# Performer attention and an MLP-mixer on one core: VectorE's maxima, reciprocals and head scalings as jobs of their own, some of the scalings on other engines, and a new order

## The chip, the core and the metric

The kernel runs on one core of a Trainium2 chip. The core has a matrix engine (TensorE, "PE", with its weight loads as "PEld"), three engines for elementwise work (VectorE "DVE", ScalarE "ACT", GpSimd "POOL") and a queue engine (SyncE "SP") that issues transfers. Every engine takes its instructions in the order in which the program holds them. TensorE writes its products into eight banks of PSUM, from which DVE and ACT read them.

The metric is device time of one execution in microseconds (us), the median of the runs. Before the change it is 279.47 us over three runs (279.39 to 279.99).

## The reference

Attention with random features comes first, for 8 batches of 8 heads with 576 rows of 64 numbers. Its result, 512 numbers for each row, goes through a mixer: a two-layer network over the rows and then one over the 512 channels, each with what went in added to what comes out.

```python
def phi(x):                                  # x: q or k, times 64 ** -0.25
    h = x @ omega.T - (x * x).sum(-1, keepdims=True) / 2
    return np.exp(h - h.max(-1, keepdims=True)) / np.sqrt(128)
q_p, k_p = phi(q_s), phi(k_s)
kv = np.einsum('bhsm,bhsd->bhmd', k_p, v)
num = np.einsum('bhsm,bhmd->bhsd', q_p, kv)
den = np.einsum('bhsm,bhm->bhs', q_p, k_p.sum(2))[..., None] + 1e-06
x = (num / den)                              # heads side by side: [8, 576, 512]
h = np.maximum(x.transpose(0, 2, 1) @ w_tok1, 0) @ w_tok2
u = x + h.transpose(0, 2, 1)
out = u + np.maximum(u @ w_ch1, 0) @ w_ch2
```

## The kernel before

**Tiling.** Of each batch's 576 rows, 512 lie as four blocks of 128 on the partitions; the last 64 (the tail) are handled with those of another head or batch. Products run in fp16 with fp32 sums.

**Attention** (`attention`, from L564) goes by pairs of heads. PE projects k (L699) and q (L711, tail rows L661 and L594), ACT takes the exponentials (L557). For k the row's maximum is divided out after the exponential: DVE takes the maximum over 128 features (L723, `km`), its reciprocal (L725) goes into a 65th column of `vs`, and POOL multiplies v by that column (L731, shown at the helper's L306). PE multiplies (L744, tail rows L751 or L753), a copy brings the product to SBUF (`kvsb`), and PE forms numerator and denominator of one head in one bank (L777, tail L779). The head scaling follows: DVE takes the reciprocal of the denominators, five numbers in each partition (L786), and multiplies five blocks of 64 by them (L787) into `x`. In batch 0 alone, two heads are multiplied by ACT (L799), which takes five instructions, one for each block.

**Mixer.** `token_mix` multiplies `x` by the first weights (L813, L820), a relu goes to `r`, the second product (L833) is added to `x` by DVE (L836), and a transfer on SP turns the result around (L841). Batch 0 has its own form in smaller pieces (L859 on). The tails of two batches go together (L887, DVE's sum L893). In `channel_mix` the first layer is L1120 (four matmuls and a relu for each of 12 blocks) and the second L965, for batch 0 L1155. The second layer uses a scheme with seven instead of eight products for batches 1 on, whose weight sums (`T`, L490) and operand sums (`S`, `r` at L306) DVE makes; from batch 6 on the first layer does too (L1053).

**Order.** Every piece of work is a job: `add(engine, cost, key, fn, deps, take, give)`. Nothing is scheduled when the program is built. `ORDER` is a list of job numbers, and the program is written out in exactly that order; a negative number is one 512-column matmul on zeros, which keeps PE's clock up (L1193). `SLOT` says which buffer of its ring a job takes. `MOVED` gives the engine for a job by its number, where it isn't the usual one (`engine`, L174). Relus and copies have ACT or DVE as their choice, the scaling of v POOL or DVE. Costs and keys play no part any more.

Of the kernel before, what the change touches and what calls it, by code (L numbers as in the profile page):

```python
# [9 lines left out]
FP32 = mybir.dt.float32  # L10
# [57 lines left out]
]  # L68
SLOT = (
# [110 lines left out]
def kernel(  # L180
# [12 lines left out]
    nc = tc.nc  # L193
# [28 lines left out]
    def ring(n, shape, dt, name):  # L222
        return [sb(shape, dt, f"{name}{i}") for i in range(n)]

    COUNT = {"qT": 3, "kT": 3, "v": 3, "vt": 2, "qp": 4, "kp": 4, "vs": 4, "qpt": 2, "kpt": 2, "vbd": 2,
             "kvsb": 3, "ktt": 2, "x": 3, "r1": 3, "u": 3, "uT": 3, "r3": 2, "S": 1, "V": 1, "s": 3, "o": 2, "bank": 8}
    plan = Planner(COUNT)
    place = plan.place
    engine = plan.engine
# [996 lines left out]
```

## Time and profile before

| what | us |
|---|---|
| median of three runs | 279.47 (279.39 to 279.99) |
| the profiled execution | 279.72 |
| its span, from the first instruction to the last | 277.9 |
| PE busy | 265.6 |
| DVE busy | 233.7 |
| ACT busy | 154.5 |
| POOL busy | 91.6 |
| mean granted clock of TensorE | 0.974 of full speed |

Busy time is the time in which at least one instruction of that engine ran. Matmuls overlap one another, so PE's share says that it had work and not that it ran at its peak. A wait is counted where an engine stood idle for more than 0.15 us, and is put down to the engine whose result came last.

### The profile page before, as it was taken

Reading aid. Unit: us, or ns where it says so; the run is one execution under the profiler, and the core shown is the slowest. Engines: PE = TensorE matmul, PEld = TensorE weight load, DVE = VectorE, ACT = ScalarE, POOL = GpSimd, SP = SyncE. Lnnn points to the kernel's source line nnn. Section 1 sums busy time; section 2 is a strip of 40 time slices with the busy share of each in tenths; the row PEclk is TensorE's granted clock in tenths of the full one; section 3 lists DMA queues with packets and bytes.
Section 4 is the critical chain, followed back from the end, with each engine's and each line's share of the span. In section 5 each row is a group of like instructions: output and inputs, shape, how many; then the busy total and the mean of one; then the engine's idle time right before and its main releaser. Section 6 shows DMA issues by size and latency. Waiting matters only on the chain.

```text
span 277.9 us, 6547 instructions
## 1 busy us (share of the span) xinstructions
PE 265.6 (96%) x2624; PEld 179.5 (65%) x2624; DVE 233.7 (84%) x487; ACT 154.5 (56%) x318; POOL 91.6 (33%) x115
## 2 busy tenths in 40 slices
PE   5789999999999999999999999999999999999993
PEld 2657546443657755665677646764597688888882
DVE  1698828499999889996998799999997999889992
ACT  2797994049667427644567544878835425153410
POOL 8597794007510773048006910333400000000000
PEclk9559999999999999999999999999999999999999
DMA  7999999999997999995989993970060062030125
GB/s 160 200 205 169 182 185 204 164 151 211 182 226 164 164 211 162 170 196 89 189 181 211 203 195 85 167 179 4 18 174 0 2 150 97 0 153 0 65 105 136
DMA packets 80622, 39.69 MB, mean 143 GB/s; under 512 B 63984, under 2 KB 76144, under 8 KB 80400
## 3 DMA queue, kind: packets, MB, share of 16 engines
q0 software_dynamic: 31696, 17.61, 44.0%
q1 hardware_dynamic: 47696, 18.52, 30.5%
q10 hardware_dynamic: 1200, 3.15, 3.2%
q8 instruction: 20, 0.33, 0.5%
q14 instruction: 10, 0.08, 0.1%
HBM read 35.95 MB, written 16.52 MB: 189 GB/s over the span
## 4 chain that ended last, share of the span: by engine, by line
PE 88%; DVE 4%; DMA 3%; ACT 2%; issue 1%; ACTq 0%; DVEq 0%
PE bank L965 25%; PE bank L1120 22%; PE bank L1053 9%; PE bank L833 5%; PE bank L820 5%; PE bank L1155 4%; PE bank L711 3%; PE bank L699 3%; DMA wc<-in_k_dram 3%; PE bank L777 3%; PE bank L744 2%; DVE o L954 1%; PE bank L887 1%; DVE x L787 1%; PE bank L859 1%; ACT qp L557 1%
## 5 line engine op out<-in xcount | busy, mean ns | idle before, releaser
L301 ACT ACTIVATE r<-bank 128x512 f16<-128x512 f32 (+1 forms) x82 | 46.3, 604 | 43.5 <-PE bank L1120 25.6
L1120 PE MATMUL bank<-uT,wc 128*128 128x512 f16 x280 | 67.9, 379 | 0.0
L306 POOL TENSOR_TENSOR vs<-v,vs 128x512 f16<-128x512 f16 x32 | 34.3, 1072 | 79.5 <-DVE vs L725 49.8
L1120 PEld LDWEIGHTS <-wc 128*128 128x128 f16 x280 | 24.8, 98 | 25.7 <-issue 2.6
L965 PEld LDWEIGHTS <-r 128*128 128x128 f16 x384 | 36.7, 98 | 6.9 <-issue 1.3
L557 ACT ACTIVATE qp<-bank 128x512 f16<-128x512 f32 x64 | 36.6, 624 | 8.0 <-PE bank L711 5.2
L557 ACT ACTIVATE kp<-bank 128x512 f16<-128x512 f32 x64 | 36.5, 617 | 7.2 <-PE bank L699 7.0
L723 DVE TENSOR_REDUCE km<-kp 128x8 f16<-128x1024 f16 x32 | 38.5, 1205 | 0.6 <-ACT kp L557 0.4
L787 DVE TENSOR_TENSOR x<-bank,rc 128x320 f16<-128x320 f32 x62 | 30.5, 492 | 2.1
L965 PEld LDWEIGHTS <-S 128*128 128x128 f16 x288 | 28.2, 98 | 5.3 <-issue 0.6
L999 POOL DMA_DIRECT2D out_dram<-o x1 | 0.7, 665 | 73.4 <-issue 73.4
L965 PE MATMUL bank<-T,r 128*128 128x256 f16 x192 | 23.8, 273 | 0.0
L965 PE MATMUL bank<-wc,r 128*128 128x256 f16 x192 | 23.6, 273 | 0.0
L965 PE MATMUL bank<-T,S 128*128 128x256 f16 x192 | 23.6, 273 | 0.0
L303 DVE TENSOR_SCALAR r<-bank 128x512 f16<-128x512 f32 (+1 forms) x26 | 17.1, 663 | 7.5 <-PE bank L820 4.9
L954 DVE TENSOR_TENSOR o<-u,bank 128x512 f32<-128x512 f16 x28 | 19.0, 679 | 2.8 <-PE bank L965 2.6
L836 DVE TENSOR_TENSOR u<-x,bank 128x512 f16<-128x512 f16 x28 | 17.6, 680 | 0.5 <-ACT r L297 0.5
L777 PEld LDWEIGHTS <-qp 128*128 128x128 f16 x256 | 13.7, 100 | 6.2 <-issue 0.2
L954 DVE TENSOR_TENSOR o<-o,bank 128x512 f32<-128x512 f32 (+1 forms) x25 | 15.1, 612 | 2.7 <-PE bank L965 2.5
L1053 PEld LDWEIGHTS <-wc 128*128 128x128 f16 x144 | 13.8, 98 | 2.6 <-issue 0.6
L777 PE MATMUL bank<-kvsb,qp 128*128 128x65 f16 x256 | 15.0, 196 | 0.0
L711 PE MATMUL bank<-qT,omT 64*128 64x512 f16 x64 | 12.5, 410 | 1.7 <-ACT qT L297 1.7
(151 smaller groups left out, 470.5 us busy)
## 6 DMA issues: line engine op xcount, KB each, us to landing
out_dram<-o SPq DMA_DIRECT2D x10, 512.0 KB, 2.9
q<-in_q_dram POOLq DMA_DIRECT2D x6, 576.0 KB, 9.6
wc<-in_moe_w_ch_dram POOLq DMA_DIRECT2D x4, 768.0 KB, 10.8
k<-in_k_dram POOLq DMA_DIRECT2D x6, 512.0 KB, 7.8
v<-in_v_dram POOLq DMA_DIRECT2D x6, 512.0 KB, 10.0
out_dram<-o ACTq DMA_DIRECT2D x4, 512.0 KB, 2.7
r<-in_q_dram POOLq DMA_DIRECT2D x4, 288.0 KB, 7.1
v<-in_v_dram POOLq DMA_DIRECT2D x4, 256.0 KB, 9.5
```

The source lines that it names most:

```text
L301: nc.scalar.activation(out=out, in_=in_, func=AF.Relu)
L306: (nc.gpsimd if eng == "POOL" else nc.vector).tensor_tensor(**kw)
L557: nc.scalar.activation(out=out, in_=in_, func=AF.Exp, bias=0.0, scale=1.0)
L711: nc.tensor.matmul(ps[e], omT[half[e]], t[half[e], 2 * hp : 2 * hp + 2, 0:R], start=True, stop=True)
L723: nc.vector.reduce_max(out=mx, in_=kpv, axis=AX.X)
L777: nc.tensor.matmul(ps[:, k, j * 65 : (j + 1) * 65], st, s[:, i, 0 : D + 1], start=True, stop=True)
L787: nc.vector.tensor_tensor(out=t_x[place("x", b)][:, :, (2 * hp + hs[0]) * D : (2 * hp + hs[0] + n) * D].rearrange("p j (i d) -> p i j d", ...
L836: nc.vector.tensor_tensor(out=t_u[place("u", b)][:, j, :], in0=t_x[place("x", b)][:, j, :], in1=bank(n), op=ALU.add)
L954: nc.vector.tensor_tensor(out=o, in0=a, in1=ps, op=ALU.add)
L965: nc.tensor.matmul(ps[:, j * DH : (j + 1) * DH], a[:, cb, j * P : (j + 1) * P], w[:, cb, :], start=(bank_of(b, j0) not in held and j == j0 ...
L1053: nc.tensor.matmul(ps[:, 2 * P * t : 2 * P * t + 2 * P], a_[:, k, cb * P : (cb + 1) * P], m[:, :, k, :], start=(begin and t == 0 and k == ...
L1120: nc.tensor.matmul(ps, wc1[:, db, cb * P : (cb + 1) * P], moving(db), start=(db == 0), stop=(db == ND - 1))
```

## The change

Five things are altered in the code.

1. DVE's two or three instructions for one thing, which stood together in one job, become jobs of their own: the maximum of k and its reciprocal, the maximum, reciprocal and mask product of the tail rows, the reciprocal of a head's denominators and the head scaling, and the two halves of the sum for two batches' tails. Others can now stand between them.
2. Each head scaling can go to DVE or ACT. In batch 0 the same two heads have ACT as their usual engine; with `MOVED`, 24 of the 64 heads are ACT's (2 before) and 40 DVE's.
3. Seven of 32 scalings of v are DVE's; all were POOL's.
4. There are four buffers for the maxima (`km`) instead of two, and six for a head's reciprocals (`rc`) instead of four of twice the size.
5. `ORDER`, `SLOT` and `MOVED` are new throughout. Ten warming matmuls are left of 13. Ten more relus from PSUM are DVE's, and ACT has six more in SBUF.

```diff
-             "kvsb": 3, ... "o": 2, "bank": 8}
+             "kvsb": 3, ... "o": 2, "km": 4, "rc": 6, "bank": 8}
...
             def km(hp=hp):
                 kpv = t_kp[place("kp", (b, hp))].rearrange("p c e m -> p (c e) m")
-                mx, vs = t_km[hp % 2], t_vs[place("vs", (b, hp))]
-                nc.vector.reduce_max(out=mx, in_=kpv, axis=AX.X)
+                nc.vector.reduce_max(out=t_km[place("km", (b, hp))], in_=kpv, axis=AX.X)
+            j_m = add("DVE", 1.2, at_["km"], km, deps=je, take=[("km", (b, hp))])
+            def km_rec(hp=hp):
                 with nc.allow_low_precision(reason="fp16 operand of the matmul"):
-                    nc.vector.reciprocal(out=vs[:, :, D], in_=mx)
-            j_m = add("DVE", 1.4, at_["km"], km, deps=je, take=[("vs", (b, hp))])
+                    nc.vector.reciprocal(out=t_vs[place("vs", (b, hp))][:, :, D], in_=t_km[place("km", (b, hp))])
+            j_m = add("DVE", 0.2, at_["km"], km_rec, deps=[j_m], take=[("vs", (b, hp))], give=[("km", (b, hp))])
...
-                    nc.vector.reciprocal(out=rc, in_=ps[:, :, :, D])
-                    nc.vector.tensor_tensor(
...
+                def rec(where=where, rc_of=rc_of):
+                    nc.vector.reciprocal(out=rc_of(), in_=where()[:, 0, 0 : 5 * 65].rearrange("p (j d) -> p j d", d=65)[:, :, D])
...
+                j_r = add("DVE", 0.22, kno - 0.3, rec, deps=[j_n], take=[n_rc])
+                e_no = engine(*("ACT", "DVE") if b == 0 and BY["no"][2 * hp + hs[0]] == "A" else ("DVE", "ACT"))
+                def num_out(hp=hp, i=hs[0], where=where, rc_of=rc_of, e_no=e_no):
+                    to = t_x[place("x", b)][:, :, (2 * hp + i) * D : (2 * hp + i + 1) * D]
+                    ps = where()[:, 0, 0 : 5 * 65].rearrange("p (j d) -> p j d", d=65)[:, :, 0:D]
+                    if e_no == "DVE":
+                        nc.vector.tensor_tensor(out=to, in0=ps, in1=rc_of().unsqueeze(2).broadcast_to((P, NJ + 1, D)), op=ALU.mult)
+                        return
+                    for j in range(NJ + 1):
+                        nc.scalar.activation(out=to[:, j], in_=ps[:, j], func=AF.Copy, scale=rc_of()[:, j : j + 1])
+                last_x.append(add(e_no, 0.62, kno, num_out, deps=[j_r], take=[("x", b)], give=[at, n_rc]))
```

What moves is seen only in the engines' own order. In the rows below a line number, the operation, what it writes and reads (with the buffer's number) and the shape follow one another. Line numbers of the changed kernel are nine to some 25 higher: its L801 is L786 or L796 here, its L809 L787, its L812 L799, its L736 and L740 the maximum L723 and its reciprocal L725, its L499 L490, its L306, L312 and L315 the helpers' L297, L303 and L306.

The first place is DVE where batch 0's first heads are scaled (`x_118`), some 19 us into the span. Before:

```order
L297 CAST kvsb_116<-bank_66 128x2x65
L297 COPY kT_88<-bank_68 128x576
L297 COPY kT_88<-bank_70 128x576
L796 RECIPROCAL rc_141<-bank_66 128x5
L786 RECIPROCAL rc_143<-bank_69 128x5
L787 TENSOR_TENSOR x_118<-bank_69,rc_143 128x5x64
L786 RECIPROCAL rc_143<-bank_64 128x5
L787 TENSOR_TENSOR x_118<-bank_64,rc_143 128x5x64
```

After:

```order
L315 TENSOR_TENSOR vs_105<-v_90,vs_105 128x8x64
L801 RECIPROCAL rc_143<-bank_63 128x5
L801 RECIPROCAL rc_144<-bank_70 128x5
L740 RECIPROCAL vs_106<-km_137 128x8
L306 COPY kT_88<-bank_68 128x576
L809 TENSOR_TENSOR x_118<-bank_63,rc_143 128x5x64
L801 RECIPROCAL rc_145<-bank_64 128x5
L809 TENSOR_TENSOR x_118<-bank_64,rc_145 128x5x64
```

A copy of `kvsb` and one of `kT` have left DVE, a scaling of v has come, and the reciprocal of a maximum and a copy now stand between a head's reciprocal and its scaling.

The second place is DVE where batch 2's attention begins, some 64 us into the span, with the weight sums `T` (L490). Before:

```order
L723 TENSOR_REDUCE km_135<-kp_99 128x8
L725 RECIPROCAL vs_103<-km_135 128x8
L490 TENSOR_TENSOR T<-wc_81,T 128x1536
L490 TENSOR_TENSOR T<-wc_81 128x1536
L303 TENSOR_SCALAR r_131<-bank_63 128x512
L723 TENSOR_REDUCE km_135<-kp_101 128x8
L725 RECIPROCAL vs_106<-km_135 128x8
L723 TENSOR_REDUCE km_134<-kp_102 128x8
L725 RECIPROCAL vs_104<-km_134 128x8
L303 TENSOR_SCALAR r_131<-bank_64 128x512
L490 TENSOR_TENSOR T<-wc_81,T 128x1536
```

After:

```order
L740 RECIPROCAL vs_104<-km_134 128x8
L740 RECIPROCAL vs_106<-km_135 128x8
L902 TENSOR_TENSOR ut<-x_118,bank_67 64x512
L736 TENSOR_REDUCE km_136<-kp_102 128x8
L312 TENSOR_SCALAR r_131<-bank_70 128x512
L499 TENSOR_TENSOR T<-wc_81,T 128x1536
L306 CAST kvsb_115<-bank_68 128x2x65
L740 RECIPROCAL vs_105<-km_136 128x8
L736 TENSOR_REDUCE km_137<-kp_101 128x8
L312 TENSOR_SCALAR r_131<-bank_69 128x512
```

One weight sum is left here, behind the first relu `r_131`, with a copy of `kvsb` right behind it; two have moved up, into batch 1's token mix.

The third place is ACT where batch 2's heads (`x_120`) are scaled among the relus `r_131` of batch 1's channel mix. Before:

```order
L301 ACTIVATE r_131<-bank_68 128x512
L301 ACTIVATE r_131<-bank_66 128x512
L297 CAST kvsb_117<-bank_63 128x2x65
L297 CAST kvsb_116<-bank_64 128x2x65
L301 ACTIVATE r_131<-bank_70 128x512
L301 ACTIVATE r_131<-bank_67 128x512
L297 CAST kvsb_115<-bank_65 128x2x65
```

After:

```order
L310 ACTIVATE r_131<-bank_70 128x512
L812 ACTIVATE x_120<-bank_65,rc_146 128x64 x5
L812 ACTIVATE x_120<-bank_67,rc_148 128x64 x5
L306 CAST kvsb_115<-bank_65 128x2x65
L310 ACTIVATE r_131<-bank_68 128x512
L310 ACTIVATE r_131<-bank_70 128x512
L812 ACTIVATE x_120<-bank_67,rc_143 128x64 x5
L310 ACTIVATE r_131<-bank_66 128x512
```

Three heads of batch 2, five instructions each, now stand between these relus.

More of the change, by code (lines that the diff above doesn't have):

```diff
@@ L76 @@
 )
 MOVED = {
-43: "ACT", 51: "ACT", 54: "ACT", 60: "ACT", 63: "ACT", 65: "ACT", 75: "DVE", 85: "ACT", 129: "ACT", 139: "DVE", 141: "DVE", 145: "ACT", 147: "DVE",
-163: "ACT", 169: "DVE", 171: "ACT", 175: "DVE", 179: "ACT", 190: "ACT", 194: "ACT", 228: "ACT", 242: "DVE", 256: "DVE", 265: "DVE", 278: "DVE", 280:
-"DVE", 286: "DVE", 300: "DVE", 324: "ACT", 399: "DVE", 426: "DVE", 428: "DVE", 432: "DVE", 434: "DVE", 484: "DVE", 498: "DVE", 552: "DVE", 556: "DVE",
-562: "DVE", 593: "ACT", 594: "ACT", 634: "DVE", 662: "DVE", 690: "DVE", 692: "DVE", 700: "DVE", 702: "DVE", 768: "DVE", 796: "DVE", 864: "ACT", 972:
@@ L82 @@
-"DVE", 988: "DVE", 1003: "ACT", 1105: "DVE", 1125: "DVE", 1127: "DVE", 1134: "DVE", 1157: "DVE", 1165: "ACT", 1203: "DVE", 1233: "DVE", 1242: "ACT",
-1244: "ACT", 1282: "SP", 1283: "SP", 1285: "ACT", 1286: "SP", 1287: "ACT", 1288: "SP", 1289: "ACT", 1290: "SP", 1291: "ACT", 1292: "SP",
+43: "ACT", 51: "ACT", 54: "ACT", 56: "ACT", 59: "ACT", 62: "ACT", 65: "ACT", 66: "ACT", 75: "DVE", 86: "ACT", 106: "DVE", 120: "ACT", 135: "DVE", 137:
+"ACT", 149: "DVE", 159: "ACT", 165: "DVE", 167: "DVE", 173: "ACT", 189: "ACT", 194: "ACT", 206: "DVE", 225: "DVE", 230: "ACT", 242: "DVE", 244: "ACT",
@@ new lines @@
+247: "ACT", 261: "DVE", 264: "ACT", 267: "ACT", 278: "DVE", 289: "DVE", 305: "DVE", 313: "DVE", 319: "DVE", 323: "DVE", 349: "ACT", 381: "ACT", 395:
+"DVE", 418: "ACT", 432: "ACT", 459: "DVE", 461: "DVE", 463: "DVE", 467: "DVE", 473: "DVE", 532: "ACT", 558: "DVE", 560: "DVE", 563: "ACT", 575: "DVE",
+580: "ACT", 583: "ACT", 586: "DVE", 604: "DVE", 610: "DVE", 620: "DVE", 647: "ACT", 675: "DVE", 714: "ACT", 717: "ACT", 726: "DVE", 728: "DVE", 731:
+"ACT", 737: "DVE", 752: "DVE", 758: "DVE", 762: "DVE", 768: "DVE", 862: "ACT", 865: "ACT", 876: "DVE", 879: "ACT", 901: "DVE", 909: "DVE", 911: "DVE",
@@ new lines @@
+915: "DVE", 979: "ACT", 1013: "ACT", 1027: "DVE", 1057: "DVE", 1069: "DVE", 1078: "DVE", 1088: "DVE", 1090: "DVE", 1098: "ACT", 1099: "ACT", 1100:
+"ACT", 1101: "ACT", 1111: "DVE", 1154: "DVE", 1160: "ACT", 1174: "ACT", 1191: "ACT", 1205: "DVE", 1211: "ACT", 1216: "DVE", 1237: "DVE", 1246: "DVE",
+1251: "DVE", 1265: "DVE", 1276: "ACT", 1278: "ACT", 1315: "DVE", 1331: "DVE", 1345: "DVE", 1353: "ACT", 1354: "ACT", 1355: "ACT", 1356: "ACT", 1393:
+"ACT", 1394: "SP", 1395: "SP", 1397: "ACT", 1398: "SP", 1399: "ACT", 1400: "SP",
@@ L225 @@
     COUNT = {"qT": 3, "kT": 3, "v": 3, "vt": 2, "qp": 4, "kp": 4, "vs": 4, "qpt": 2, "kpt": 2, "vbd": 2,
-             "kvsb": 3, "ktt": 2, "x": 3, "r1": 3, "u": 3, "uT": 3, "r3": 2, "S": 1, "V": 1, "s": 3, "o": 2, "bank": 8}
+             "kvsb": 3, "ktt": 2, "x": 3, "r1": 3, "u": 3, "uT": 3, "r3": 2, "S": 1, "V": 1, "s": 3, "o": 2, "km": 4, "rc": 6, "bank": 8}
     plan = Planner(COUNT)
@@ L271 @@
     t_o = ring(COUNT["o"], [P, 2, DM], FP32, "o")
-    t_km = ring(2, [P, 8], FP16, "km")
+    t_km = ring(COUNT["km"], [P, 8], FP16, "km")
     t_kmt = ring(2, [P, 4], FP16, "kmt")
@@ L275 @@
     t_rct = ring(2, [P, 4], FP16, "rct")
-    t_rc = ring(4, [P, 2, NJ + 1], FP32, "rc")
+    t_rc = ring(COUNT["rc"], [P, NJ + 1], FP32, "rc")
     nat = {}
@@ L562, in vbd_of @@
         return first_vbd[:, b] if b < NPE else t_vbd[place("vbd", b)]
+    kt_parts = {}
     def attention(b, key, step):
@@ L629, in attention, with kt_red, kt_rec, kt_vb @@
                 j_kte.append(add("ACT", 0.3, kkt, kt_exp, deps=[j_kt], take=[("kpt", b)], give=[("bank", (n_kt, e))]))
-            def kt_max():
-                kp = t_kpt[place("kpt", b)].rearrange("p g e m -> p (g e) m")
-                mx, rc, vb = t_kmt[b % 2], t_rct[b % 2], vbd_of(b)
-                nc.vector.reduce_max(out=mx, in_=kp, axis=AX.X)
+            def kt_red():
+                nc.vector.reduce_max(out=t_kmt[b % 2], in_=t_kpt[place("kpt", b)].rearrange("p g e m -> p (g e) m"), axis=AX.X)
+            j_ktm = add("DVE", 0.7, kkt + 0.01, kt_red, deps=[*j_kte, *kt_parts.get(b - 2, [])])
+            def kt_rec():
                 with nc.allow_low_precision(reason="fp16 operand of the matmul"):
-                    nc.vector.reciprocal(out=rc, in_=mx)
+                    nc.vector.reciprocal(out=t_rct[b % 2], in_=t_kmt[b % 2])
+            j_ktr = add("DVE", 0.2, kkt + 0.01, kt_rec, deps=[j_ktm])
+            def kt_vb():
                 nc.vector.tensor_tensor(
-                    out=vb[:, :, 0:nh, D],
-                    in0=rc.unsqueeze(2).broadcast_to((P, 4, nh)),
+                    out=vbd_of(b)[:, :, 0:nh, D],
+                    in0=t_rct[b % 2].unsqueeze(2).broadcast_to((P, 4, nh)),
                     in1=msk.unsqueeze(1).broadcast_to((P, 4, nh)),
@@ L641, in kt_max @@
                 )
-            j_ktm = add("DVE", 1.2, kkt + 0.01, kt_max, deps=[*j_kte, j_msk], take=[("vbd", b)] if dma_in else [])
+            j_ktm = add("DVE", 0.2, kkt + 0.01, kt_vb, deps=[j_ktr, j_msk], take=[("vbd", b)] if dma_in else [])
+            kt_parts[b] = [j_ktr, j_ktm]
             def vbd():
@@ L781, in attention @@
                           give=[("qp", (b, hp)), ("kvsb", (b, hp)), ("qpt", b)])
-                def num_out(hp=hp, hs=hs, where=where):
-                    n = len(hs)
-                    ps = where()[:, :, 0 : 5 * 65].rearrange("p i (j d) -> p i j d", d=65)
-                    rc = t_rc[2 + hp % 2][:, hs[0] : hs[0] + n]
-                    nc.vector.reciprocal(out=rc, in_=ps[:, :, :, D])
-                    nc.vector.tensor_tensor(
-                        out=t_x[place("x", b)][:, :, (2 * hp + hs[0]) * D : (2 * hp + hs[0] + n) * D].rearrange("p j (i d) -> p i j d", i=n),
-                        in0=ps[:, :, :, 0:D],
-                        in1=rc.unsqueeze(3).broadcast_to((P, n, NJ + 1, D)),
-                        op=ALU.mult,
-                    )
@@ L793, in attention @@
-                kno = HEAD["no"][2 * hp + hs[0]] if b == 0 else at_["no"]
-                if b == 0 and BY["no"][2 * hp + hs[0]] == "A":
-                    def rec(hp=hp, i=hs[0], where=where):
-                        nc.vector.reciprocal(out=t_rc[hp % 2][:, i], in_=where()[:, 0, 0 : 5 * 65].rearrange("p (j d) -> p j d", d=65)[:, :, D])
-                    def scale(hp=hp, i=hs[0], where=where):
-                        for j in range(NJ + 1):
-                            nc.scalar.activation(out=t_x[place("x", b)][:, j, (2 * hp + i) * D : (2 * hp + i + 1) * D],
-                                                 in_=where()[:, 0, j * 65 : j * 65 + D], func=AF.Copy, scale=t_rc[hp % 2][:, i, j : j + 1])
-                    j_r = add("DVE", 0.22, kno - 0.3, rec, deps=[j_n])
-                    last_x.append(add("ACT", 1.1, kno, scale, deps=[j_r], take=[("x", b)], give=[at]))
-                else:
-                    last_x.append(add("DVE", 0.1 + 0.52 * len(hs), kno, num_out, deps=[j_n], take=[("x", b)], give=[at]))
+                n_rc = ("rc", (b, hp, hs[0]))
@@ new lines, in rc_of @@
+                def rc_of(n_rc=n_rc):
+                    return t_rc[place(*n_rc)]
+                def rec(where=where, rc_of=rc_of):
+                    nc.vector.reciprocal(out=rc_of(), in_=where()[:, 0, 0 : 5 * 65].rearrange("p (j d) -> p j d", d=65)[:, :, D])
+                kno = HEAD["no"][2 * hp + hs[0]] if b == 0 else at_["no"]
+                j_r = add("DVE", 0.22, kno - 0.3, rec, deps=[j_n], take=[n_rc])
+                e_no = engine(*("ACT", "DVE") if b == 0 and BY["no"][2 * hp + hs[0]] == "A" else ("DVE", "ACT"))
@@ L889, in token_tail, with uadd @@
         j1 = add("PE", mm(2, 512), key, go, deps=[*jr, j_w2], take=[("bank", n)], give=[("r1", 2 * pair_), ("r1", 2 * pair_ + 1)], rows="cols")
-        def uadd():
-            for o in range(2):
-                s = half[o]
+        j2 = []
+        for o in range(2):
+            def uadd(o=o, s=half[o]):
                 nc.vector.tensor_tensor(out=t_ut[s, pair_], in0=t_x[place("x", 2 * pair_ + o)][s, NJ, :], in1=bank(n)[s], op=ALU.add)
-        j2 = add("DVE", 1.36, key, uadd, deps=[j1], give=[("bank", n), ("x", 2 * pair_), ("x", 2 * pair_ + 1)])
+            j2.append(add("DVE", 0.69, key, uadd, deps=[j1], give=[("bank", n), ("x", 2 * pair_ + o)]))
         return j2
@@ L1187 @@
         channel_mix(b, float(b), uT)
-    tails = [tail_transpose(i, 7.1 + 0.1 * i, [j, ld["kT", B - 1]]) for i, j in enumerate(tails)]
+    tails = [tail_transpose(i, 7.1 + 0.1 * i, [*j, ld["kT", B - 1]]) for i, j in enumerate(tails)]
     channel_mix(B, float(B), tails)
```

12 lines of the change are left out of this document (6 added, 6 removed), and 93 rows, old and new, of the table ORDER.

## The prediction

> **What bounds the kernel now.** I read the page first, its busy shares.
>
> ```profile
> span 277.9 us, 6547 instructions
> ...
> PE 265.6 (96%) x2624; PEld 179.5 (65%) x2624; DVE 233.7 (84%) x487; ACT 154.5 (56%) x318; POOL 91.6 (33%) x115
> ```
>
> The tensor engine (PE) is busy for 265.6 of 277.9 us. So the question for every edit is which of the remaining 12.3 us (277.9 - 265.6) it can reach, or whether it opens new ones. The second view cuts the span into stages. Columns: length, then busy us and count for PE, its weight loads, VectorE (DVE), ScalarE (ACT) and GpSimd (POOL), then granted clock and DMA; the last rows lack POOL's work.
>
> ```profile
> 20.00:32.70 12.70, 12.23 (x206) 9.36 (x205) 10.49 (x25) 10.18 (x30) 8.97 (x13) 0.96 1.17 179
> 32.70:66.00 33.30, 33.29 (x262) 16.22 (x260) 22.60 (x50) 18.30 (x38) 14.83 (x18) 1.00 1.21 191
> 66.00:100.00 34.00, 33.52 (x327) 20.84 (x327) 30.99 (x58) 22.35 (x47) 13.67 (x17) 1.00 1.00 165
> 100.00:150.00 50.00, 50.00 (x487) 31.68 (x484) 45.25 (x99) 28.01 (x58) 17.58 (x21) 1.00 1.02 182
> 150.00:205.00 55.00, 54.73 (x556) 34.31 (x555) 51.39 (x105) 37.61 (x78) 20.24 (x22) 1.00 0.71 128
> 205.00:226.00 21.00, 20.39 (x185) 15.73 (x183) 18.43 (x41) 8.22 (x14) 0.00 (x0) 1.00 0.20 53
> 226.00:274.00 48.00, 47.53 (x435) 42.29 (x433) 43.05 (x88) 16.68 (x30) 0.67 (x1) 1.00 0.23 82
> ```
>
> PE's idle time from 20 to 274 us is length minus busy, row by row: 0.47 + 0.01 + 0.48 + 0.00 + 0.27 + 0.61 + 0.47 = 2.3 us. The other 10 us lie before 20 and after 274 us. From 66 to 205 us DVE is busy for 127.6 of 139 us (30.99 + 45.25 + 51.39): it runs level with PE, while ACT has 88.0 of 139. The third view says for whom PE waited (us, times, longest):
>
> ```profile
> PE bank L661 <- DVE r L303: 0.5, 1, 0.5
> PE bank L859 <- DVE x L787: 0.5, 1, 0.5
> PE bank L965 <- DVE o L954: 0.5, 1, 0.5
> ...
> PE bank L699 <- DVE x L787: 0.2, 1, 0.2
> PE bank L1053 <- ACT bank L297: 0.2, 1, 0.2
> ```
>
> These five are all of PE's waits behind 20 us. Four of them end with DVE, and 1.9 us is their sum. The engine the change relieves is therefore the right one, but what it can give back is small.
>
> **The change part by part.** Its instructions, by shape. Each row is a group: count, then busy us and mean ns of one.
>
> ```profile
> L306 POOL TENSOR_TENSOR vs<-v,vs 128x512 f16<-128x512 f16 x32 | 34.3, 1072 | 79.5 <-DVE vs L725 49.8 <-PE bank L965 13.7 <-issue 7.7
> L787 DVE TENSOR_TENSOR x<-bank,rc 128x320 f16<-128x320 f32 x62 | 30.5, 492 | 2.1
> ...
> L836 DVE TENSOR_TENSOR u<-x,bank 128x512 f16<-128x512 f16 x28 | 17.6, 680 | 0.5 <-ACT r L297 0.5
> L303 DVE TENSOR_SCALAR r<-bank 128x512 f16<-128x512 f32 x24 | 16.2, 683 | 6.7 <-PE bank L820 4.9 <-PE bank L1053 1.0 <-PE bank L1120 0.8
> ...
> L799 ACT ACTIVATE x<-bank,rc 128x64 f16<-128x64 f32 x10 | 2.3, 322 | 0.2 <-DVE rc L796 0.2
> ...
> L306 DVE TENSOR_TENSOR S<-S,r 128x512 f16<-128x512 f16 x3 | 1.3, 422 | 0.1
> ...
> L303 DVE TENSOR_SCALAR r<-r 128x512 f16<-128x512 f16 x4 | 1.1, 286 | 0.0
> ```
>
> Head scalings: 62 were DVE's and 2 ACT's; now 40 and 24. DVE loses 22 x 0.492 = 10.8 us. ACT runs a head as five instructions, 2.3 / 2 = 1.15 us a head, so it gains 22 x 1.15 = 25.3 us and stands near 180 of 278 us.
>
> Scalings of v: 7 leave POOL (7 x 1.07 = 7.5 us) for DVE. No row shows this one on DVE. The bounds are 0.42 (the same shape, plain operands) and 0.68 (512 elements with an operand in PSUM). The head scaling, whose second operand is repeated along the row as here, runs at 320 elements in 0.492, which is the speed of the slower bound; I take 0.68, so 7 x 0.68 = 4.8 us (2.9 at the lower bound).
>
> Relus: DVE takes 10 more from PSUM of 512 elements (20 to 27 whole, 4 to 7 split), 10 x 0.683 = 6.8 us, and gives ACT one of 256 elements (at most 0.4) and six in SBUF (four of 512 elements at 0.286, two of 1024 at no more than twice that, 2.0 together). Three copies leave DVE and three others come. DVE's sum: -10.8 + 4.8 + 6.8 - 0.4 - 2.0 = -1.6 us. By load alone DVE is hardly relieved.
>
> The separated jobs do more. The next rows are DVE in order of time (start, length):
>
> ```profile
> 21.59 0.18 DVE L786 RECIPROCAL rc<-bank 128x5 f32<-128x5 f32 x1
> 21.80 0.49 DVE L787 TENSOR_TENSOR x<-bank,rc 128x320 f16<-128x320 f32 x1
> ...
> 26.17 0.18 DVE L796 RECIPROCAL rc<-bank 128x5 f32<-128x5 f32 x1
> 26.27 0.15 DVE L786 RECIPROCAL rc<-bank 128x5 f32<-128x5 f32 x1
> ```
>
> A reciprocal whose result the next instruction reads holds DVE for 0.21 us (21.59 to 21.80); one followed by something unrelated for 0.10 (26.17 to 26.27). In the new order 44 of 64 reciprocals of heads are followed by something unrelated (2 before), and 20 of 32 maxima of k (none before). At 0.1 us each (an estimate for the maxima, from the reciprocals) that is 6.2 us more. So DVE has some 8 us less to do (1.6 + 6.2), about 4 of them in its full stretch from 66 to 205 us (half of the span). The Trainium skill, "VectorE: DVE Perf Modes", rules for kernel authors, says the opposite of chained operations: the drain comes after each one anyway, and only their count matters. By it the 6.2 us would be nought; the trace's 0.21 against 0.10 speaks against it.
>
> What this gives PE, stage by stage. In 20 to 32.7 us PE waits 0.5 us for the first head's scaling; now a group of L699, one of L530 and the L777 of another two heads stand ahead of the first L859, work that PE has to do anyway. The order has 2 warming matmuls there instead of 5. A full matmul is 0.216 us (1.73 / 8 in the next rows), and the old ones partly filled waits, so I count half of 3 x 0.216: 0.3. Sum -0.8, and -0.5 if DVE's new v scaling, queued ahead of these heads, takes 0.3 of it back. I take -0.6.
>
> ```profile
> 60.62 1.83 PE bank L1155 x8
> ...
> 64.81 1.73 DVE T L490
> ...
> 66.58 0.70 DVE r L303
> ...
> 103.97 1.73 PE bank L1120 x8
> ```
>
> At 66 us two passes over the second layer's weights (T, L490) stand before a relu (L303) that frees PE's bank. In the new order three of the four run earlier, in batch 1's token mix (one before), where DVE was busy for only 22.60 of 33.30 us, and the last stands behind such a relu. This wait goes: -0.5. Late next would be a copy of kvsb that now stands right behind the last pass; between the L744 that it waits for and the L777 that reads it PE has eight matmuls of L1120, 1.73 us, as long as the pass. Without that cover it would cost up to the 1.73. From 150 to 226 us PE idles 0.27 + 0.61 = 0.9 us behind head scalings and output sums on DVE; I take two thirds away: -0.6.
>
> Against it: groups of 64-row matmuls are entered or left 74 times instead of 72 in PE's order. Eight full matmuls take 1.73 us, and 1.83 right behind such a group, so 0.1 each: +0.2. New waits: PE's order is another at nearly every step and 2.3 us of idle time is very little, so I allow +0.4 (between 0 and the rivals below). POOL's and SP's loads keep their order within a few places; POOL has 7.5 us less ahead of them, which is worth nothing while PE waits for no load behind 20 us. The first 18 us of PE's order are unchanged, and the end keeps its form: matmuls of L965, a sum on DVE, a store.
>
> Sum: -0.6 - 0.5 - 0.6 + 0.2 + 0.4 = -1.1 us on the profiled execution's 279.72 (span 277.9 and 1.8 around it), 278.6. That execution is 0.25 above the median of the runs shown (279.47, from 279.39 to 279.99), so in their measure 278.4.
>
> **The rivals.** *ACT holds PE's banks: slower.* A head on ACT keeps it for 1.15 us, and relus queued behind that free PE's banks; four matmuls of L1120 need only 0.86 us. Fifteen such heads lie in batches 2 to 6, among the relus of the batch before. For: ACT's stretch from 150 to 205 us is already at 37.61 of 55, and PE waits for no relu of ACT now, so there is everything to lose. Against: there are eight banks, and seven of the relus are now DVE's. If the 0.29 us by which a head outlasts four matmuls reach PE each time, that is 15 x 0.29 = 4.3 us: 279.5 - 1.1 + 4.3 = 282.7. It decides from 1.1 / 15 = 0.07 us a head.
>
> *The waits only move: no change.* DVE's relief is off PE's path, which is 99% full from 20 to 274 us, and new single waits replace the five old ones: +1.1 more than I allowed, 279.5. The skill's rule on chained operations would lead here too.
>
> *All waits go.* PE idles for nothing behind 20 us and the three warming matmuls count in full: 2.3 + 0.6 - 0.2 = 2.7 us, 276.8. For: both DVE and ACT have free time now in every stage. Against: the last 0.47 (226 to 274) hangs on sums that are not touched.
>
> **How the numbers follow.** Forecast (0.6 to 2.0 us gained) 0.40, all waits 0.10, no change 0.15, ACT or another new wait slower 0.35. About 0.2% (0.56 us) is what a measurement of this kernel tells from no change. So faster 0.50, same 0.15, slower 0.35. The likeliest is 278.4, its own range 277.5 to 278.9. For 8 in 10 the range goes from 276.9, at the edge of the rival in which all waits go, up to 281.6, which is 0.21 of these 0.29 us a head in the slower rival (279.5 - 1.1 + 15 x 0.21).
>
> **What would show it.** In the changed profile: DVE near 230 us busy, ACT near 180, POOL near 84. PE's waits behind 20 us below 1.5 us in sum; no wait of L661 for the relu, none of L859 for head scalings. The v scaling on DVE at 0.68 us, 0.42 if I chose the wrong bound. I am wrong if PE's wait list names ACT's relus or head scalings with more than 1 us, if L744 or L777 waits for kvsb near 70 us, or if the first L1120 group starts later than 32.7 us.

## The result, and the profile after

The changed kernel takes 278.18 us (median of six runs, 277.51 to 278.79), beside 279.52 for the kernel before in the same session: a ratio of 0.9949, with a 95% interval of 0.9932 to 0.9967. That is 1.34 us less; 278.4 was forecast. The profiled execution is the slowest of the six, 278.79 with a span of 277.0.

The page of the changed kernel, its busy shares:

```profile
span 277.0 us, 6623 instructions
...
PE 264.7 (96%) x2621; PEld 178.9 (65%) x2621; DVE 225.5 (81%) x475; ACT 177.4 (64%) x426; POOL 83.4 (30%) x107
```

DVE stands 8.2 us lower than before (233.7), ACT 22.9 higher, POOL 8.2 lower (besides the seven scalings of v, a copy of `ktt` has gone from POOL to DVE). The stages again (length, then busy us and count for PE, its weight loads, DVE, ACT and POOL, then clock and DMA):

```profile
20.00:32.70 12.70, 12.18 (x213) 9.22 (x209) 9.93 (x28) 11.79 (x30) 7.98 (x10) 0.94 1.25 192
32.70:66.00 33.30, 33.17 (x274) 16.61 (x269) 21.86 (x46) 23.12 (x59) 12.54 (x16) 1.00 1.16 200
66.00:100.00 34.00, 34.00 (x327) 20.47 (x326) 28.92 (x60) 25.43 (x64) 13.90 (x17) 1.00 1.15 191
100.00:150.00 50.00, 50.00 (x489) 32.45 (x487) 44.73 (x94) 34.11 (x90) 13.62 (x18) 1.00 0.95 160
150.00:205.00 55.00, 54.83 (x565) 34.05 (x563) 49.81 (x108) 40.67 (x101) 19.27 (x21) 1.00 0.69 127
205.00:226.00 21.00, 21.00 (x181) 16.43 (x179) 18.24 (x38) 11.69 (x29) 0.00 (x0) 1.00 0.22 55
```

From 20 to 226 us PE now idles 0.52 + 0.13 + 0.00 + 0.00 + 0.17 + 0.00 = 0.8 us, where the same rows of before give 1.8. For whom it waits behind 20 us (us, times, longest):

```profile
PE bank L792 <- DVE kT L306: 0.3, 1, 0.3
PE bank L974 <- DVE o L963: 0.2, 1, 0.2
PE bank L713 <- ACT x L812: 0.2, 1, 0.2
```

The five waits of before (1.9 us) are down to three (0.7 us). The one on the relu of L303 is gone, and so is that of the first token mix on a head scaling. Only 0.2 us names a head on ACT.

What lies outside these stages has to be taken out before the spans are compared. The first matmul behind the unchanged start, in the changed kernel and then in the one before (start, length, wait):

```profile
15.61 1.04 PE L725 MATMUL bank<-qT,omT 64*128 64x512 f16 x4 [1.71 <-ACT qT L306]
```

```profile
15.04 1.04 PE L711 MATMUL bank<-qT,omT 64*128 64x512 f16 x4 [1.72 <-ACT qT L297]
```

The changed kernel's execution was 0.57 us late here; in its list of waits the largest of the start is one of 2.4 us for an input transfer. The last matmuls, of the one before and of the changed kernel:

```profile
272.71 0.82 PE L965 MATMUL bank<-T,r 128*128 128x256 f16 x6
```

```profile
270.80 1.47 PE L974 MATMUL bank<-wc,S 128*128 128x256 f16 x12
```

PE ends at 273.53 (272.71 + 0.82) and at 272.27 (270.80 + 1.47), 1.26 earlier. From there to the span's end it is 4.4 us before and 4.7 now, the last sums and stores. So the span's 0.9 us are 1.26 less 0.34; without the late start, PE would have ended some 1.8 us earlier.

### The profile page after: what moved, and what is told of

It reads as the page before. It is cut to its first block, busy times and chain, and to the rows that moved or that the text cites. A ratio compares the mean times of both kernels' runs of the same rounds, so it can differ in the third digit from the quotient of the medians.

```text
span 277.0 us, 6623 instructions
## 1 busy us (share of the span) xinstructions
PE 264.7 (96%) x2621; PEld 178.9 (65%) x2621; DVE 225.5 (81%) x475; ACT 177.4 (64%) x426; POOL 83.4 (30%) x107
## 4 chain that ended last, share of the span: by engine, by line
PE 83%; DMA 8%; DVE 3%; POOL 2%; ACT 1%; issue 1%; POOLq 0%
PE bank L974 26%; PE bank L1129 21%; PE bank L1062 10%; PE bank L829 5%; PE bank L842 4%; PE bank L1164 4%; DMA k<-in_k_dram 3%; PE bank L759 3%; DMA wc<-in_moe_w_ch_dram 3%; DMA r<-in_k_dram 3%; PE bank L792 3%; PE bank L713 2%; PE bank L725 2%; ACT qp L566 1%; DVE u L845 1%
## 5 line engine op out<-in xcount | busy, mean ns | idle before, releaser
L1129 PE MATMUL bank<-uT,wc 128*128 128x512 f16 x280 | 67.4, 379 | 0.1
L310 ACT ACTIVATE r<-bank 128x512 f16<-128x512 f32 (+1 forms) x73 | 42.5, 609 | 25.5 <-PE bank L1129 11.6
L315 POOL TENSOR_TENSOR vs<-v,vs 128x512 f16<-128x512 f16 x25 | 26.3, 1059 | 69.4 <-DVE vs L740 46.2
L1129 PEld LDWEIGHTS <-wc 128*128 128x128 f16 x280 | 25.6, 98 | 25.1 <-issue 0.6
L566 ACT ACTIVATE kp<-bank 128x512 f16<-128x512 f32 x64 | 35.6, 613 | 6.1 <-PE bank L713 6.0
L736 DVE TENSOR_REDUCE km<-kp 128x8 f16<-128x1024 f16 x32 | 38.1, 1198 | 1.5 <-ACT kp L566 1.5
L974 PEld LDWEIGHTS <-S 128*128 128x128 f16 x288 | 27.4, 98 | 4.9 <-issue 1.3
L812 ACT ACTIVATE x<-bank,rc 128x64 f16<-128x64 f32 x120 | 26.9, 332 | 2.4 <-DVE rc L801 2.2
L312 DVE TENSOR_SCALAR r<-bank 128x512 f16<-128x512 f32 (+1 forms) x35 | 23.5, 672 | 4.3 <-PE bank L1062 2.2
L809 DVE TENSOR_TENSOR x<-bank,rc 128x320 f16<-128x320 f32 x40 | 18.7, 480 | 0.7
L801 DVE RECIPROCAL rc<-bank 128x5 f32<-128x5 f32 x64 | 10.3, 180 | 8.8 <-PE bank L794 8.6
L315 POOL TENSOR_TENSOR vbd<-vt,vbd 128x512 f16<-128x512 f16 x6 | 6.3, 1051 | 36.8 <-DVE vbd L649 18.4
```

The costliest lines, as they stand in the source:

```text
L310: nc.scalar.activation(out=out, in_=in_, func=AF.Relu)
L312: nc.vector.tensor_relu(out=out, in_=in_)
L315: (nc.gpsimd if eng == "POOL" else nc.vector).tensor_tensor(**kw)
L566: nc.scalar.activation(out=out, in_=in_, func=AF.Exp, bias=0.0, scale=1.0)
L736: nc.vector.reduce_max(out=t_km[place("km", (b, hp))], in_=kpv, axis=AX.X)
L812: nc.scalar.activation(out=to[:, j], in_=ps[:, j], func=AF.Copy, scale=rc_of()[:, j : j + 1])
```

## The experiments

Each time is a median beside the kernel before in the same session; "against the changed kernel" means the difference of the two differences from before, with the changed kernel's as -1.34.

| kernel | us | before beside it | ratio (95%) |
|---|---|---|---|
| old_order_apart | 279.33 | 279.36 | 1.0001 (0.9992 to 1.0009) |
| new_order_chained | 280.66 | 279.36 | 1.0051 (1.0038 to 1.0063) |
| old_order_act_heads | 288.37 | 279.37 | 1.0311 (1.0286 to 1.0337) |
| old_order_new_engines | 296.86 | 279.36 | 1.0641 (1.0618 to 1.0665) |
| new_order_old_engines | 283.44 | 279.36 | 1.0159 (1.0141 to 1.0178) |
| after_heads_dve | 280.85 | 279.65 | 1.0050 (1.0037 to 1.0062) |
| after_relus_old | 281.86 | 279.37 | 1.0082 (1.0067 to 1.0096) |
| after_vs_pool | 277.89 | 279.65 | 0.9943 (0.9931 to 0.9955) |
| before_T_early | 279.15 | 279.65 | 0.9985 (0.9974 to 0.9997) |
| before_three_warms_less | 279.35 | 279.65 | 0.9989 (0.9978 to 1.0000) |
| before_T_early_warms_less | 278.93 | 279.37 | 0.9986 (0.9976 to 0.9995) |
| after_vs_pool_no_late_warm | 279.13 | 279.37 | 0.9981 (0.9965 to 0.9997) |

Kernels called "old order" are the changed kernel's code with the list of before: a job that the change has split stands there as its parts, one right behind the other, so that every engine has the rows of before, unless said otherwise. Their lines are up to three higher than those of the changed kernel (a head on ACT is L815 for L812).

### Reciprocals apart, or beside what they belong to

**old_order_apart**: the order of DVE alone, at 52 places, such as

```diff
  L739 TENSOR_REDUCE km_134<-kp_99
- L743 RECIPROCAL vs_103<-km_134
  L309 COPY qT_84<-bank_69
+ L743 RECIPROCAL vs_103<-km_134
...
+ L804 RECIPROCAL rc_145<-bank_64
  L812 TENSOR_TENSOR x_118<-bank_69,rc_144
- L804 RECIPROCAL rc_145<-bank_64
  L812 TENSOR_TENSOR x_118<-bank_64,rc_145
```

> The order, the engines and the 13 warming matmuls of before, with only the reciprocals taken apart: 32 of heads one DVE instruction earlier, 20 of maxima of k one later. My theory: DVE is held 52 x 0.1 = 5.2 us less, some of the 1.9 us that PE waits behind 20 us goes, 279.0 to 279.4. The rival, by which setting apart is worth nothing: 279.5.

Measured: no change, within 0.1%. The page of this run:

```profile
PE 265.9 (96%) x2624; PEld 179.3 (65%) x2624; DVE 226.7 (82%) x487; ACT 154.3 (56%) x318; POOL 92.2 (33%) x115
```

DVE is busy for 7.0 us less than before (233.7), more than the 5.2 expected: the 32 reciprocals that were moved leave 52 heads' pairs apart, not 32, since the one ahead is parted too, so that 72 pairs in all give some 0.1 us each. In the measured time it is worth nothing. The 279.33 lies in my range only because before took 279.36 here; beside that the theory fell. PE's order is the same in both kernels, so their profiles can be compared matmul by matmul: PE of this run gains 0.6 us near 67 us, 0.4 near 184 and 0.3 near 209 on that of before, and loses 0.5 near 33 and 0.3 near 129. What DVE's lighter load gives at some places is lost at others; each is read from one execution.

**new_order_chained**: the reverse, in the changed kernel.

```diff
  L736 TENSOR_REDUCE km_137<-kp_101
+ L740 RECIPROCAL vs_106<-km_137
  L315 TENSOR_TENSOR vs_103<-v_91,vs_103
  L315 TENSOR_TENSOR vs_104<-v_91,vs_104
- L740 RECIPROCAL vs_106<-km_137
```

> The changed kernel with 18 reciprocals of heads and 20 of maxima of k moved back right beside the instruction they belong with on DVE; all else in place. My theory, that a result read by the next instruction costs about 0.1 us: DVE is held 38 x 0.1 = 3.8 us longer and a part of it reaches PE, 278.4 to 279.0. The rival, by which only the count of instructions matters: 278.2, and the starts behind such reciprocals no later than behind the others.

Measured: 280.66, which is 2.6 us against the changed kernel, far over the 0.2 to 0.8 that I gave it. DVE is busy for 230.6 us instead of 225.5, so 5.1 us for 38 pairs. The same stretch of DVE, in this run and then in the changed kernel (start, length):

```profile
178.58 1.21 DVE L736 TENSOR_REDUCE km<-kp 128x8 f16<-128x1024 f16 x1
179.89 0.21 DVE L740 RECIPROCAL vs<-km 128x8 f16<-128x8 f16 x1
180.01 0.51 DVE L315 TENSOR_TENSOR S<-r,S 128x768 f16<-128x768 f16 x1
180.43 0.29 DVE L306 CAST kvsb<-bank 128x130 f16<-128x130 f32 x1
```

```profile
177.50 1.17 DVE L736 TENSOR_REDUCE km<-kp 128x8 f16<-128x1024 f16 x1
178.58 0.62 DVE L315 TENSOR_TENSOR S<-r,S 128x768 f16<-128x768 f16 x1
179.13 0.28 DVE L306 CAST kvsb<-bank 128x130 f16<-128x130 f32 x1
179.33 0.20 DVE L740 RECIPROCAL vs<-km 128x8 f16<-128x8 f16 x1
```

Two things differ. A maximum followed by its own reciprocal holds DVE for 1.31 us (178.58 to 179.89), one followed by a sum for 1.08 (177.50 to 178.58). And the reciprocal stands behind the copy `kvsb` in the changed kernel, ahead of it here. PE waits for that copy (at 180.78, the longest of its waits behind 20 us):

```profile
PE bank L792 <- DVE kvsb L306: 0.7, 1, 0.7
```

Here, being apart lets an instruction go first for which PE waits. Compared matmul by matmul (PE's order is the same), this run falls behind the changed kernel by 2.7 us from 28 us to the end: 0.9 at this copy, and the rest in steps of 0.1 to 0.5 near 47, 70, 91, 110, 151 and 187 us. So this place is a third of it. How much of the whole is the hold and how much the order, this run does not separate, since it changes both.

### Engines and order, one without the other

**old_order_act_heads** and **old_order_new_engines**: in the old order, `MOVED` of the changed kernel for the 24 head scalings, and then for everything.

```diff
+ 230: "ACT", 247: "ACT", 264: "ACT", 267: "ACT", 381: "ACT",
...
+ 1174: "ACT", 1191: "ACT", 1211: "ACT",
```

> The order of before with one thing moved: the changed kernel's 24 heads are scaled by ACT, all other engines as before. With all engines moved this order took 17.5 us more. My theory, by the prediction's rival that ACT holds PE's banks: a head outlasts four matmuls by 0.29 us, 22 heads more, 22 x 0.29 = 6.4 us or more where relus queue behind them, 284 to 288, with PE waits for x and relus of ACT. The rival, that the relus and v scalings on DVE carry the 17.5: 281 or less.

> The order of before, each reciprocal still right ahead of what reads it, and all 13 warming matmuls; only the engines are the changed kernel's (24 heads on ACT, 7 scalings of v and ten more relus on DVE). My theory, that the gain comes from single places of the order and from three warming matmuls less: no gain, 279.5 to 280.5, since ACT's heads stand where nothing was laid out for them. The rival, that work taken off DVE is what counts: 278.9 or less, with PE's waits for DVE behind 20 us under 1 us.

Measured: 9.0 us and 17.5 us more than before. The first is just above the range that I gave it; the expectation of the second, no gain, was far off. The 9.0 are 0.41 us for each of the 22 heads that ACT has more; in the profile PE's waits behind 20 us name ACT's heads with 3.6 us, and relus and heads on DVE with another 2.1. How it happens can be read where batch 5's heads fall between relus, first on ACT and then on PE, in old_order_act_heads:

```profile
168.07 1.14 ACT L815 ACTIVATE x<-bank,rc 128x64 f16<-128x64 f32 x5 [0.71 <-DVE rc L804]
169.07 0.62 ACT L313 ACTIVATE r<-bank 128x512 f16<-128x512 f32 x1
169.55 1.17 ACT L815 ACTIVATE x<-bank,rc 128x64 f16<-128x64 f32 x5
```

```profile
165.32 3.62 PE L1132 MATMUL bank<-uT,wc 128*128 128x512 f16 x16
169.26 1.02 PE L1132 MATMUL bank<-uT,wc 128*128 128x512 f16 x4 [0.32 <-ACT x L815]
170.77 0.39 PE L728 MATMUL bank<-qT,omT 64*128 64x512 f16 x2 [0.49 <-ACT x L815]
```

The first head ends at 169.21 (168.07 + 1.14) and PE's next matmuls, which need its bank, start at 169.26; the second ends at 170.72, and PE goes on at 170.77. The new order seems to give these heads more time. Counted in the two orders by the matmuls between (0.216 us for 512 columns), PE has a median of 3.2 us of work between a head's product and its next use of that bank where ACT scales the head, and less than 2 us for 2 of the 24. In the old order ACT's 24 heads have 2.4 us, and 6 of them less than 2; but the means, 3.5 and 3.3, are close. No run tests this count by itself.

**new_order_old_engines**: the changed kernel's `ORDER`, all engines as before. **after_heads_dve**, **after_relus_old** and **after_vs_pool** undo one part of that each: the heads; the relus, copies and sums (and which queue issues a store); the scalings of v.

```diff
- 106: "DVE", 230: "ACT", 247: "ACT", 264: "ACT",
...
- 1174: "ACT", 1191: "ACT", 1211: "ACT",
```

> The changed kernel's order with the engines of before (2 heads on ACT, all scalings of v on POOL, the relus as before). My theory: the order counts on what its engines do at each place, so part of the gain goes: 278.5 to 279.5, with PE waits for head scalings on DVE in batches 2 to 6. Rival one, the order alone brings it: 278.2 as the changed kernel. Rival two, the engines bring it: 279.5 or more.

> The changed kernel with the engines of before for the head scalings alone (62 on DVE, 2 on ACT); order, v scalings and relus as changed. With all engines of before this order took 283.4. My theory: the heads are most of these 5.2 us, since 22 x 0.48 = 10.6 us more stand on DVE at places where PE waits for it: 281.0 to 283.5, with PE's excess between 66 and 205 us. The rival, that the relus' places carry it: 278.7 or less.

> The changed kernel with the relus, copies and sums between DVE and ACT (and which queue issues a store) as before; heads and v scalings as changed. All engines of before cost 5.2 us in this order, the heads 2.8 of them, the v scalings none. If the parts add up: 278.2 + 2.4 = 280.6, and 280 to 281.5. The rival, that relus alone can be anywhere and only with the heads on DVE do they cost: 278.0 to 278.8.

> The changed kernel with all scalings of v back on POOL; all else as changed. My theory: POOL is idle for most of the span and takes 1.06 us against 0.68 on DVE, so the time hardly moves: 278.0 to 278.7. The rival, that in these seven places the product that reads vs is next on PE: 279.2 or more, with PE waits of L759 for vs on POOL.

Measured against the changed kernel: all engines +5.4 us, the heads alone +2.5, the relus alone +3.8, the scalings of v -0.4. The parts add up (5.9 beside 5.4). For all engines my range was far too low: the order alone not only brings no gain, with the old engines it is 4.1 us slower than before. The number is that of the second rival (the engines bring it), but the same engines in the old order cost 17.5 us, so neither brings it alone. The heads came out just under the range that I gave them, the relus above theirs, and the rival by which relus can be anywhere fell. The seven scalings of v on DVE bring nothing: without them the kernel is at 0.9943, with them at 0.9949, and the intervals overlap. The profiles agree: from 25 us to the end PE of after_vs_pool runs 1.02 to 1.05 us ahead of the changed kernel's, matmul by matmul, without a step; that is a difference of the two starts.

### Single places

**before_T_early**: three passes over the second layer's weights (jobs 34 to 36), and nothing else.

```diff
- ... 264, 263, 178, 265, 328, 184, 266, 179, 34, 272, ... 388, 35, ...
+ ... 264, 263, 178, 34, 35, 36, 265, 328, 184, 266, 179, 272, ... 388, ...
```

> Before with three of the four passes over the second layer's weights (T) moved up on DVE to where DVE is idle for 3.57 us, ahead of 54.67 us. My theory: PE's wait for the relu at 67 us goes, and each moved pass takes 0.95 us, since POOL scales no v beside it (1.81 where it did): 0.5 us less than before, 278.9. The rival, that PE merely waits elsewhere: 279.36, with a new wait of 0.3 us or more between 66 and 100 us.

Measured: 0.15% less (0.03 to 0.26%), about 0.4 us, near the 0.5 of the sum. The wait for the relu near 67 us is gone from the list and no wait between 66 and 100 us has come for it. That alone shows little, since it is missing in the profiles of old_order_apart and before_three_warms_less too, where the passes stand as before; but matmul by matmul PE is level with before (0.1 us ahead) up to 66 us, 0.65 ahead at 72 and 0.6 ahead at the end. Each pass takes 0.95 us there:

```profile
50.95 0.95 DVE L491 TENSOR_TENSOR T<-wc 128x1536 f16<-128x1536 f16 x1
51.93 0.96 DVE L491 TENSOR_TENSOR T<-wc,T 128x1536 f16<-128x1536 f16 x1
52.81 0.95 DVE L491 TENSOR_TENSOR T<-wc 128x1536 f16<-128x1536 f16 x1
```

**before_three_warms_less**: `-6`, `-7` and `-6` are left out of `ORDER`.

```diff
- 140, 223, 206, -6, 199, 148, ... 224, 32, 198, -7, 207, 149, -6, 247, 233,
+ 140, 223, 206, 199, 148, ... 224, 32, 198, 207, 149, 247, 233,
```

> Before with the last three of its five late warming matmuls left out and nothing else. They are work that the output does not need. My theory: half of their 3 x 0.216 us stood on PE's path, so 0.3 us less than before, some 279.05 beside 279.36. Rival one, they only fill waits: 279.36. Rival two, they keep the clock up: slower, with a granted clock under 0.96 from 20 to 33 us.

Measured: 0.3 us less, 0.11%, with an interval that touches nought. The size is that of the theory; that it is more than noise isn't settled. In its profile PE waits 0.24 us at 63.88 and 0.38 at 94.60 for the transposed `u`, which it does not in before's, so part of what was saved went there. The granted clock did not fall in this run behind 20 us (1.00 from 20 to 32.7): the second rival is not seen here.

**before_T_early_warms_less**: both.

> Before with both single edits: three passes of T moved up and three late warming matmuls less. If they add up, 0.4 + 0.3 = 0.7 us under before, 278.7 to 278.9, which is half of the change's gain without a new order. The rival, that PE waits elsewhere once both are gone: 279.1 or more.

Measured: 0.44 us less, between the sum (0.7) and the rival (0.3 or less); the interval goes from 0.1 to 0.7 us and does not settle it. Together they are at most half of the change's gain.

**after_vs_pool_no_late_warm**: the two late `-2` of the changed kernel left out, with v on POOL.

```diff
- ... 81, 31, 56, -2, 121, 62, 124, 122, -2, 125, 100, ...
+ ... 81, 31, 56, 121, 62, 124, 122, 125, 100, ...
```

> The changed kernel with all scalings of v on POOL and without its last two late warming matmuls (work that the output does not need). By the three left out of before, at half of 0.216 us each: 0.2 less than the 277.9 with POOL's scalings, 277.7, the fastest so far. The rival, that these two only fill a wait: 277.9.

Measured: 279.13, 1.4 us above my figure; its runs spread from 277.71 to 279.78. The stages around the place where the two stood, in this run and then in after_vs_pool (columns as above):

```profile
18.00:20.00 2.00, 1.41 (x43) 0.97 (x40) 0.28 (x2) 2.00 (x7) 2.00 (x4) 0.86 1.17 211
20.00:22.00 2.00, 1.31 (x25) 1.06 (x25) 1.59 (x6) 1.84 (x8) 1.66 (x3) 1.00 1.10 207
22.00:24.00 2.00, 1.99 (x39) 1.77 (x39) 1.75 (x4) 1.92 (x5) 2.00 (x4) 0.50 1.17 212
24.00:26.00 2.00, 2.00 (x33) 1.77 (x32) 1.28 (x4) 0.84 (x4) 1.93 (x3) 0.65 1.27 197
```

```profile
18.00:20.00 2.00, 2.00 (x44) 1.44 (x41) 0.16 (x1) 2.00 (x7) 2.00 (x4) 1.00 1.15 209
20.00:22.00 2.00, 1.65 (x32) 1.22 (x30) 1.63 (x7) 1.78 (x7) 1.69 (x3) 1.00 1.12 208
22.00:24.00 2.00, 1.91 (x53) 1.65 (x53) 1.93 (x6) 2.00 (x6) 2.00 (x3) 1.00 1.16 210
24.00:26.00 2.00, 2.00 (x44) 1.79 (x41) 1.93 (x7) 1.85 (x6) 1.88 (x3) 1.00 1.26 193
```

Without the two, PE idles 0.59 + 0.69 = 1.28 us from 18 to 22 us, 0.35 with them. Then the granted clock drops to 0.50 and 0.65, and from 22 to 26 us PE gets through 72 matmuls instead of 97. The 1.00 in the first row of after_vs_pool was not measured, for its trace has no entry of the clock before 20.22; four matmuls of 65 columns take 0.42 us there at 19.64 and 0.28 at 20.97, so the clock was low and rose, and then it held. Matmul by matmul, the run without the two is 0.1 us behind up to 22 us, 1.27 at 25, and as much to the end: the fall makes 1.15 of the 1.34 us by which these two executions differ. In them the two fillers were no work on the path: they fill waits. It is one execution of each, and the fastest of the eleven runs, 277.71, is as fast as with them; so the drop seems not to come each time.

No run beats the changed kernel by more than its interval; after_vs_pool, 277.89, is level with it.

## Why the prediction came out right, and which of its steps did not

The time, 278.18, lies 0.2 from the forecast and in its own range. Step by step:

**The bound** was read rightly: a kernel whose PE idles some 2 us could give back about that. One row was misread. The 0.47 us of the stage from 226 to 274 us lay behind PE's last matmul (273.53 + 0.47), so it was no idle time to be had, and the 2.3 us were 1.8. Only the rival in which all waits go rested on it.

**20 to 32.7 us, -0.6.** The waits, half of it, brought nothing: the head's 0.5 us went, but 0.3 for `kT` and 0.2 for a head on ACT came in the same microseconds, and the idle time is 0.52 for 0.47. What came is three warming matmuls less. Where waits are counted apart these stand in full, 0.65 us; leaving three out of before gave 0.3, which is not clear of noise. So the size may be right, but not by the terms of which I made it up. By the letter, a sign of being wrong came true here: the first L1129 starts at 33.87, later than 32.7. It was no sign of a loss: 0.57 us are the late start, and three matmuls of L1135, which now stand ahead of it from 33.21 on, are 0.66.

**66 us, -0.5.** Right in mechanism: the stage's idle time fell from 0.48 to 0.00, and the single move brought 0.4 in before. The feared wait for `kvsb` did not come. What I had not seen is why the pass was so long: 1.81 us beside POOL's scaling of v, 0.95 elsewhere. The changed kernel's last pass (69.02 to 69.97, 0.95 us) meets no POOL instruction.

**150 to 226 us, -0.6.** 0.27 + 0.61 became 0.17 + 0.00: 0.7 us.

**Against it, +0.2 and +0.4.** The new waits are the three above, 0.7 us; two of them are those that ate the first term, and the third (0.2) replaces a longer one of the same kind. The 0.2 for groups of 64-row matmuls was not measured by itself. With the waits at -1.0 (20 to 226 us), three matmuls less (0.65), the late start (+0.57) and the end (+0.34), the span should be 0.8 shorter; it is 0.9. So PE gained more than the 1.1 of the sum, some 1.8 us in this execution, and a start and an end that the sum does not have took 0.9 of it back. That the number came within 0.2 is in part luck.

**Load and the separated jobs.** DVE fell by 8.2 us; the sum gave 1.6 + 6.2 = 7.8 (the 230 that I named as a mark was looser than that). Yet the step "the separated jobs do more" led nowhere as I used it: 7.0 us off DVE in the old order left the time as it was. The places count, and in the new order they count for more than I gave (2.6 us for 38 pairs). The 0.1 us for a maximum was too little; it is 0.2 (1.31 against 1.08). The rule of the Trainium skill, "VectorE: DVE Perf Modes", rules for kernel authors, that only the number of operations matters, does not agree with these rows. By its effect on the time it held in the old order; in the new one the hold and the order are not separated.

**The scaling of v on DVE** takes 0.68 us in six of seven cases, the bound I chose. The seventh takes 1.28 beside POOL, so the group's mean is 769 ns:

```profile
L315 DVE TENSOR_TENSOR vs<-v,vs 128x512 f16<-128x512 f16 x7 | 5.3, 769 | 0.0
```

**The rival "ACT holds PE's banks"** was a real mechanism. In the old order it cost 9.0 us, 0.41 a head, of the size of the 0.29 that I gave it, though the profile puts only 3.6 us of waits to ACT's heads by name. In the new order it did not happen (0.2 us of waits). That the new order leaves these heads more time is the likely reason; it is argued from the count above, not shown. I gave the rival 0.35 without that count, which stood in the two orders, so that it stayed away was not something the prediction had worked out.

What makes up the rest of the gain, beyond the 0.4 us that two single edits bring in the old order, is not to be split into parts: the heads, the relus and the separation, each taken back alone, cost 2.5 to 3.8 us, and of those tried in the old order the separation brings nothing and the heads cost 9 us. That order and engines only fit each other is what these runs show; which few of the places make the gain stays open.

## What to carry to other kernels

In a kernel whose order is written out, an engine's load says little: 7 us off a busy engine brought nothing, and the same moved work cost 17.5 us in one order and saved 5.4 in another. Price a change by PE's listed waits, by what frees each bank, and by how much PE has to do before it wants that bank again. Before a filler matmul is left out, look not only at the time that it takes but at the idle time which that leaves and at the clock in the microseconds behind it.

## What the runs showed of the hardware

**DVE and POOL hold each other up.** The pass T of before at 66 us, on DVE and then POOL's instruction beside it:

```profile
63.91 0.91 DVE L490 TENSOR_TENSOR T<-wc,T 128x1536 f16<-128x1536 f16 x1
64.73 1.81 DVE L490 TENSOR_TENSOR T<-wc 128x1536 f16<-128x1536 f16 x1
```

```profile
64.24 1.49 POOL L306 TENSOR_TENSOR vs<-v,vs 128x512 f16<-128x512 f16 x1
```

POOL's scaling took 1.49 us instead of its mean of 1.07 while the first pass ran to 64.82; the second pass took 1.81 instead of 0.95, and POOL ended at 65.73, which leaves it 0.81 alone. The Trainium skill, "SBUF — State Buffer", who interferes with whom, says that a DVE instruction with two inputs in SBUF contends with a POOL instruction that reads SBUF, and calls the pair of ports that they share an exclusive lock. These rows agree.

**The clock can fall after little idle time.** In after_vs_pool_no_late_warm the 1.28 us of idle time from 18 to 22 us were followed by a clock of 0.50. The longest piece of it stands ahead of this row of PE:

```profile
19.64 0.28 PE L792 MATMUL bank<-kvsb,qp 128*128 128x65 f16 x4 [0.54 <-ACT qp L566]
```

It is not the only execution. In all fourteen traces the times between changes of the clock are whole multiples of 3.41 us. The next rows take such a stretch at full clock and the one behind it, in old_order_apart, after_vs_pool_no_late_warm and old_order_new_engines (columns as above):

```profile
13.63:17.05 3.42, 1.51 (x16) 0.51 (x12) 3.39 (x6) 3.42 (x8) 2.71 (x4) 1.00 1.13 208
17.05:20.46 3.41, 3.34 (x63) 2.44 (x62) 2.79 (x8) 3.41 (x10) 2.90 (x4) 0.50 1.16 203
18.57:21.99 3.42, 2.15 (x63) 1.78 (x58) 1.59 (x6) 3.26 (x11) 3.08 (x5) 1.00 1.13 210
21.99:25.40 3.41, 3.39 (x56) 3.17 (x55) 2.63 (x8) 2.41 (x6) 3.41 (x6) 0.50 1.17 202
239.12:242.54 3.42, 2.25 (x22) 1.87 (x20) 3.06 (x6) 1.03 (x1) 0.00 (x0) 1.00 0.80 153
242.54:245.95 3.41, 3.41 (x34) 3.06 (x32) 2.83 (x6) 2.35 (x5) 0.00 (x0) 1.00 0.65 268
```

PE is idle for 1.91, 1.27 and 1.17 us in the first row of each pair; behind the first two the clock is 0.50, behind the third it stays at 1.00. The traces have eleven such falls ahead of PE's last matmul, each behind a stretch with 1.27 to 2.41 us of idle time in which no single wait is longer than 1.84, and none behind a stretch with 1.17 us or less. The last rise of the clock lies anywhere from 17.80 to 25.40 us, so the same waits can fall into one stretch or into two.

The Trainium skill, "TensorE: Matmul & The Clock Gate", why this matters for your kernels, asks only, against a drop of the clock, that no gap exceed some 3 us; these rows do not agree.
